# Convolution spectra of a Trainium2 kernel: the last two slices' products and inverses placed beside the down product, and four more slices transformed with eight residues

## The chip, the cores and the metric

The kernel runs on one core of one Trainium2 chip, in one launch. The metric is the device time of that launch in microseconds (us). The engines are named as in the profile: PE (TensorE, matrix products and transposes), DVE (VectorE), ACT (ScalarE), POOL (GpSimd) and SP (SyncE); SP, ACT and POOL also issue DMAs, each from a queue of its own that is worked off in order. PSUM is the memory that PE writes to, and SBUF is where all other tiles lie.

## The reference, cut to what matters

The kernel computes an output and the gradients of nine inputs. S is 2048 rows, D is 1024 columns, F is 3584.

```python
xn = layernorm(q)                              # rows of S x D
k_shift[t] = sum_j k_pad[t + j] * shift_k[.., ks-1-j]   # 4 taps, per column
kv  = k_shift * v
y   = irfft(rfft(kv padded to 2S) * rfft(ssm_k padded to 2S))[:S] + kv * ssm_D
s   = xn_A * y                                 # xn_A is the layer norm again
h   = (xn @ w_gate) * (xn @ w_up)              # S x F
g   = silu(h @ w_down)                         # the "down product"
out = q + s * g
# and the gradients of all inputs but B_x for a given grad_out
```

The long convolution runs column by column over all 2048 rows. The kernel does it as a discrete Fourier transform: PE multiplies pieces of the data by sine and cosine tables, and DVE combines the pieces.

## The kernel before, in words

**Stages.** PE is given one long row of work. First the gate and up products (`gu_unit`, matmuls into `psg` at L671): 14 slabs of 256 columns of F, each in four chunks of four row tiles. Then the down product (`bm_mm`, L1034, into `psbm`): 16 row tiles of 128 rows, each 28 units of two 128x512 matmuls. Then the gradients: `dh_half` (L1482) with `dw_slab` (L1499), `dwd_mm` (L1582) and `dx_part` (L1644).

**The convolution beside them.** `conv_forward` is a generator. It works through eight slices of 128 columns (`ds` 0 to 7) and gives, at each `yield`, an estimate of the DVE time of the piece just recorded. `make_pump` takes from it as much as a planned fraction allows: `tick` is called after each `psg` group and pumps up to a share that grows with a counter over `NT` ticks. So `NT` sets how far the convolution has come at a given chunk of the gate and up products. While `PIN` is set, the DVE instructions stay in the order in which they were recorded.

For a slice the generator does this: transform kv (`transform(ds, 0)`), transform the filter (`transform(ds, 1)`), multiply the spectra (`product`), invert (`inv_dft`, or `inv8` for the slices in `INV8`), and one slice later `tail` does the last matmuls of the inverse (`inv_quad`, L455, two groups per slice into `psI`) and stores the rows into `YFd`. For every two slices `shift` computes `k_shift` and kv; the taps lie broadcast over the partitions in `Wbc`.

**Two forms of the transform.** `fwd4_half` makes PE multiply two residues into each PSUM tile (16 matmuls of 128x256 for a half, 32 for a transform), and DVE needs 8 operations after it. `fwd8_half` multiplies one residue (16 matmuls for a transform) and leaves more butterflies to DVE (`fwd8`, 20 operations). The pairs in `EIGHT` (slice, 0 for kv or 1 for filter) take the second form. In both forms ACT copies `psF` to the tile `SP` and DVE reads it from there.

**What ties PE to DVE in the gate and up stage.** DVE multiplies `gut` to `hN` for each chunk. Some matmul groups later `turn_pair` transposes `hN` on PE (L565), ACT copies the result to `hT`, and SP stores it to `HTd`, from which the down product loads its left operands (`load_ht`, tiles `ht`, or the tiles U10 and U8 for rows 2 and 3). The last of these transposes stand a few us into the down product, on PE's row of work. The load of the last quarter of `w_down` into U9 waits for the store behind them.

**The down product's stage.** Rows 0 and 1 of the down product are recorded first (`bm_first`), then `late_mm(n)` records unit n of the rows from 2 on. At the units in `at`, one step of the convolution's last tail is recorded behind the matmuls, so PE reaches the last inverse matmuls there. Results of rows 2 and 3 are copied by ACT out of PSUM to a tile of the pool `bw` (`bms`), since their gates come later. After `drain()` the rows' gates follow: `gate(b)` is 9 or 10 DVE operations on 128x1024 (so, dgg, gg, sgn, sig, ds_t, dy, dbm, dxa, o_t; rows 0 and 1 have three of them done earlier), 2 sigmoids on ACT and 4 stores of 256 KB on POOL's queue. It needs 3 loads of 256 KB (do_t, xn_t, yf_t) on SP's queue, each into a pair of tiles in turn (`mi`, two buffers), so that the loads of row b+2 wait for the reads of row b. Three PSUM tiles take the rows' matmuls in turn: row b can begin when row b-3 was copied out of PSUM. Copies from row 4 on go to one tile `bm`, which is free when `gg` of the row before has been computed.

Between the row loads SP's queue has the loads of the next `ht` (1.75 MB for two rows of the product) and transposed loads of `DBMd` into the tiles `DBMT` (L1425), which are needed at 700 us. The rows from 12 on have their `dbm` transposed on PE instead (L1323), inside the matmuls of the next row: PE waits there for DVE's `dbm`.

**The end.** `dk_units` uses the taps a second time, beside the last stage of PE.

Of the kernel before, what the change touches and what calls it, by code (L numbers as in the profile page):

```python
# [13 lines left out]
BF16 = mybir.dt.bfloat16  # L14
# [5 lines left out]
def build_kernel(  # L20
# [11 lines left out]
    nc = tc.nc  # L32
# [94 lines left out]
    RSTN = const.tile([P, NB], F32, name="RSTN")  # L127
    Wbc = const.tile([P, 4, D], BF16, name="Wbc")

# [11 lines left out]
    def load_bcast(bsb):  # L141

        wrow = bsb.tile([1, D, 4], BF16, name="wrow")
        st(wrow[:].rearrange("p d j -> p (d j)"), A_shift_k.rearrange("(o d) j -> o (d j)", o=1))
        wtap = bsb.tile([1, 4, D], BF16, name="wtap")

        def turn(j):
            nc.gpsimd.tensor_copy(wtap[:, j, :], wrow[:, :, j])

        def spread():  # L150
            st(WTd.rearrange("(o x) -> o x", o=1), wtap[:].rearrange("p j d -> p (j d)"))
            st(Wbc[:].rearrange("p j d -> p (j d)"), bass.AP(WTd.tensor, WTd.offset, [[0, P], [1, 4 * D]]))
        return turn, spread
# [577 lines left out]
    ht_st = [None]  # L731
    EIGHT = ((0, 0), (0, 1), (6, 0), (7, 0), (7, 1))
    INV8 = (2, 4, 5, 6, 7)
# [6 lines left out]
    def conv_forward():  # L740
        S_ = conv_state

        def load_kv(dp, c):
            S_["k", dp] = krow
            if dp > 0 or c == 0:
                for i in range(2) if dp == 0 else (c,):
                    cld_k(krow[:, i], i, dp)
            if dp > 0 or c == 1:
                for i in range(2) if dp == 0 else (c,):
                    v = U[4][:, 2048 * i:2048 * i + 2048].rearrange("p (a x) -> p a x", a=8)  # L750
                    cld_v(v, i, dp * 256, 256)

        def load_h(ds):
            hrow = U[5][:, 0:2048].rearrange("p (c u r) -> p c u r", c=2, r=8)
            cld(U[5][:, 0:2048], A_ssm_k[ds * P:(ds + 1) * P, :])
            S_["h", ds] = hrow

        def shift(dp):
            kv = cx.tile([P, NB, 256], BF16, name="kv")
            S_["kvt", dp] = kv  # L760
            k = S_.pop(("k", dp))
            wb = lambda j: Wbc[:, j:j + 1, dp * 256:(dp + 1) * 256].unsqueeze(1).to_broadcast([P, 2, 8, 256])
# [12 lines left out]
            yield 2.3  # L775
# [22 lines left out]
        def tail(ds):  # L798
            G = S_.pop(("G", ds))
            if ds < 7:  # L800
                yf = cs.tile([P, NB, P], BF16, name="yf")[:]
            else:
                yf = krow[:].rearrange("p a b d -> p (a b d)")[:, 0:NB * P].rearrange("p (b d) -> p b d", b=NB)
# [63 lines left out]
        for ds in range(8):  # L867
            yield 0.5
            if ds % 2 == 1 and ds < 7:
                with tc.issue_after(S_["kst"].ins):  # L870
                    for c in range(2):
                        load_kv(ds // 2 + 1, c)
            D0 = Dz[:, ds * P:(ds + 1) * P]
            sph = []
            KX = cx.tile([P, 16, 256], BF16, name="KX")
            HX = cs.tile([P, 16, 256], BF16, name="HX", bufs=2)
# [14 lines left out]
            yield from transform(ds, int(ds > 0), sph, HX if ds else KX, room, nop1 if eight else lambda c: h_rows(ds + 1, c),  # L891
                                 behind)
            if ds == 0:
# [14 lines left out]
            sp = []  # L908

            def ahead():  # L910
                if ds < 7:
                    sp.append(half(ds + 1, kvs(ds + 1), len(sp)))
            yield from (inv8 if ds in INV8 else inv_dft)(KX, HX, cs, ahead if ds % 2 == 0 else None, ahead)
            if ds % 2 == 1:
                ahead()
# [65 lines left out]
    cnt = [-5]  # L981
    NT = 24 * 8.0 + 33

# [76 lines left out]

    def load_ht1():
        two_ = [u8(10, a=16), u8(8, a=16)]
        for f0, f1 in ((0, 8), (8, 16), (16, 24), (24, 28)):
            last = ld(two_[f0 // 16][:, f0 % 16:f0 % 16 + f1 - f0], ht_rows(1, f0, f1))
        return (lambda fc: two_[fc // 16][:, fc % 16]), last

    with tc.issue_after(wd_ld.ins):
        ht1 = load_ht1()
# [135 lines left out]
    def dk_units(ew):  # L1204
# [9 lines left out]
        def load_turned(i):  # L1214
# [8 lines left out]
            return kT, dkT  # L1223

        dk = load_rows(0)
        yield 3
        for i in range(16):
            ds, c = divmod(i, 2)
            dsl = slice(ds * P, (ds + 1) * P)
            wb = lambda j: Wbc[:, j:j + 1, dsl].to_broadcast([P, 8, P])  # L1230
            acc = ew.tile([P, 8, P], BF16, name="dka")
# [120 lines left out]
    bm_first(range(fc_, NF))  # L1352
    room = [bw.tile([P, DC, SLW], BF16, name="wdt")[:].rearrange("p (i x) f -> p i (x f)", i=2) for i in range(2)]
    bms = [out_of(pss[i], room[0][:, i]) for i in range(2)]
    first, parts = [u8(q, a=4) for q in (4, 5)]
    y_first[0] = u8(11, a=4)
    with tc.issue_after(ht2[1].ins):
        row_ld[0] = ld(y_first[0][:, :, 0:7 * P], YFd[:, 0:4, 0:7 * P])
    with tc.issue_after(row_ld[0].ins):
# [8 lines left out]
    def late_mm(n):  # L1368
        b, fc = divmod(n, NF)
        b += 2  # L1370
        if fc == 0:
            if 2 < b < 5 and done < 0:
                bms.append(out_of(ps_of[b - 1], room[1][:, b - 3]))
            ps_of[b] = (ps_bx if b % 3 == 2 else ps_bm).tile([P, D], F32, name="psbm")
        with tc.issue_after(inv_mm[0].ins) if b < 5 else nullcontext():
            return bm_mm(ps_of[b], hts[b // 2][0], b % 2, fc)

    at = (62, 69)
    for n in range(at[1] + 1):
        mm = late_mm(n)  # L1380
# [14 lines left out]
    with tc.issue_after(row_ld[0].ins):  # L1395
        ht3 = load_ht(3)
    for i in range(3):
# [8 lines left out]
    rows_in[4] = gate_rows(4, 0, 2) + gate_rows(4, 2, 3, [y_4])  # L1406
    done = at[1] + 1
    while done < 2 * NF:
        late_mm(done)
        done += 1  # L1410
    if len(bms) > 3:
        gate(3, None)
    else:
        gate(3, ps_of[3])
    for bp in range(2, 8):
        hts[bp] = load_ht(bp) if bp > 3 else (ht2, ht3)[bp - 2]
        ht_ld = hts[bp][1]
# [16 lines left out]
        for i in range(2):  # L1434
            n = (2 * bp + i - 2) * NF
            while done < n + NF:
# [371 lines left out]
```

## Time and profile before

| what | value |
|---|---|
| median of 3 runs (lowest to highest) | 1911.96 us (1911.43 to 1912.38) |
| the profiled execution's own time | 1911.63 us |
| its span, first to last instruction | 1909.9 us |
| PE busy | 1899.4 us, 11379 matmuls |
| DVE busy | 1549.7 us |
| gate and up products begin and end on PE | 8.9 and 501.3 us |
| down product begins and ends on PE | 501.2 and 700.2 us |
| granted TensorE clock | 1.000 |

The profile lists instructions by line of the kernel and by the names of the tiles. Matmuls overlap in it: a matmul of 512 columns is listed with 379 ns although the next one starts 216 ns after it, so the cost of one more or one less is read from how far apart the starts of equal matmuls lie. The windows view gives the busy time of each engine in stretches of the span, with the share of time in which the DMA engines were busy and the rate in GB/s. The timeline merges equal instructions that follow one another and puts in brackets how long the engine was idle before and what ended that.

### The profile page before, as it was taken

Reading aid. Unit: us, or ns where it says so; the run is one execution under the profiler, and the core shown is the slowest. Engines: PE = TensorE matmul, PEld = TensorE weight load, DVE = VectorE, ACT = ScalarE, POOL = GpSimd, SP = SyncE. Lnnn points to the kernel's source line nnn. Section 1 sums busy time; section 2 is a strip of 40 time slices with the busy share of each in tenths; the row PEclk is TensorE's granted clock in tenths of the full one; section 3 lists DMA queues with packets and bytes.
Section 4 is the critical chain, followed back from the end, with each engine's and each line's share of the span. In section 5 each row is a group of like instructions: output and inputs, shape, how many; then the busy total and the mean of one; then the engine's idle time right before and its main releaser. Section 6 shows DMA issues by size and latency. Waiting matters only on the chain.

```text
span 1909.9 us, 28150 instructions
## 1 busy us (share of the span) xinstructions
PE 1899.4 (99%) x11379; PEld 1013.9 (53%) x11379; DVE 1549.7 (81%) x1711; ACT 636.8 (33%) x927; POOL 332.7 (17%) x465
## 2 busy tenths in 40 slices
PE   8999999999999999999999999999999999999999
PEld 5555555545444466666666665664444444444444
DVE  8999999999988556887999999999995305788862
ACT  5765555556333233432222222222222102111121
POOL 5121211201113220001031221211212101111120
PEclk9999999999999999999999999999999999999999
DMA  9777766769769997677897798585887999989852
GB/s 298 269 263 233 251 208 223 252 211 311 241 227 307 316 314 231 209 231 233 264 277 247 231 266 258 184 286 180 230 238 181 219 206 190 194 187 190 194 166 88
DMA packets 425106, 444.34 MB, mean 233 GB/s; under 512 B 268400, under 2 KB 342796, under 8 KB 410512
## 3 DMA queue, kind: packets, MB, share of 16 engines
q1 hardware_dynamic: 367504, 239.03, 45.9%
q0 software_dynamic: 41152, 174.15, 29.0%
q10 hardware_dynamic: 16320, 29.36, 4.1%
q8 instruction: 89, 1.46, 0.3%
q14 instruction: 41, 0.34, 0.1%
HBM read 193.87 MB, written 189.84 MB: 201 GB/s over the span
## 4 chain that ended last, share of the span: by engine, by line
PE 97%; DVE 1%; ACT 1%; DMA 0%; issue 0%; SPq 0%; ACTq 0%
PE psb L1499 20%; PE psx L1644 20%; PE psg L671 19%; PE psb L1482 10%; PE psbm L1034 10%; PE psb L1582 9%; PE psF L234 3%; PE psI L455 1%; PE tr L565 1%; PE psY L1193 1%; PE psY L445 1%; PE psx L1582 1%; DVE bst L578 0%; DMA wslab<-in_B_w_gate_dram 0%; PE tr L788 0%; DVE U L212 0%
## 5 line engine op out<-in xcount | busy, mean ns | idle before, releaser
L671 PE MATMUL psg<-wslab,U 128*128 128x512 bf16 x1792 | 401.8, 379 | 3.5 <-DMA wslab<-in_B_w_gate_dram 2.1
L1499 PE MATMUL psb<-U,U 128*128 128x512 bf16 x1792 | 397.1, 379 | 0.0
L1644 PE MATMUL psx<-U,dgut 128*128 128x512 bf16 x1536 | 332.8, 379 | 0.0
L1644 PEld LDWEIGHTS <-dgut 128*128 128x128 bf16 x1792 | 175.3, 98 | 211.4
L1499 PEld LDWEIGHTS <-U 128*128 128x128 bf16 x1792 | 175.2, 98 | 198.0
L671 PEld LDWEIGHTS <-U 128*128 128x128 bf16 x1792 | 172.6, 98 | 197.2 <-issue 3.6
L1482 PE MATMUL psb<-wdt,U 128*128 128x256 bf16 x1792 | 205.6, 273 | 0.0
L1482 PEld LDWEIGHTS <-U 128*128 128x128 bf16 x1792 | 175.2, 98 | 29.2
L212 DVE TENSOR_TENSOR W<-W 128x1024 f32<-128x1024 f32 (+1 forms) x189 | 186.5, 1003 | 4.1
L1582 PE MATMUL psb<-U,U 128*128 128x512 bf16 x816 | 177.3, 379 | 0.0
L1504 ACT CAST wb<-psb 128x512 bf16<-128x512 f32 x112 | 65.6, 586 | 315.4 <-PE psb L1499 310.5
L1249 DVE SCALAR_TENSOR_TENSOR dkp<-dkT,kT 128x1024 bf16<-128x1024 bf16 (+2 forms) x64 | 78.3, 1223 | 93.1 <-DMA dkT<-DKSHd 91.4
L1034 PE MATMUL psbm<-U,ht 128*128 128x512 bf16 x672 | 146.0, 379 | 0.0
L1582 PEld LDWEIGHTS <-U 128*128 128x128 bf16 x896 | 87.4, 98 | 104.4
L673 ACT CAST gut<-psg 128x512 bf16<-128x512 f32 x156 | 91.5, 589 | 120.2 <-PE psg L671 119.7
L1676 ACT ACTIVATE dx_t<-dxn 128x1024 bf16<-128x1024 f32 x15 | 15.9, 1057 | 324.7 <-DVE dxn L212 324.7
L1034 PEld LDWEIGHTS <-ht 128*128 128x128 bf16 x672 | 65.7, 98 | 78.1
L212 DVE TENSOR_TENSOR U<-U,dht 128x2048 bf16<-128x2048 bf16 x56 | 68.3, 1220 | 46.5 <-ACT dht L1484 46.5
L1484 ACT CAST dht<-psb 128x512 bf16<-128x512 f32 x112 | 65.6, 587 | 116.4 <-PE psb L1482 116.4
L66 POOL DMA_DIRECT2D Hd<-hN x54 | 36.6, 677 | 268.9 <-DVE hN L212 258.9
L1623 ACT CAST wbs<-psb 128x512 bf16<-128x512 f32 x51 | 29.9, 586 | 145.4 <-PE psb L1582 134.3
L212 DVE TENSOR_TENSOR W<-SP 128x1024 f32<-128x1024 f32 x64 | 74.1, 1218 | 1.3 <-ACT SP L295 0.8
(263 smaller groups left out, 2342.9 us busy)
## 6 DMA issues: line engine op xcount, KB each, us to landing
U<-GUd SPq DMA_DIRECT2D x28, 1024.0 KB, 9.3
DGd<-U SPq DMA_DIRECT2D x28, 1024.0 KB, 5.8
GUd<-gut ACTq DMA_DIRECT2D x39, 512.0 KB, 5.2
out_dram<-wb SPq DMA_DIRECT2D x112, 128.0 KB, 4.8
U<-Hd SPq DMA_DIRECT2D x14, 1024.0 KB, 6.6
Hd<-hN POOLq DMA_DIRECT2D x54, 256.0 KB, 4.5
HTd<-hT SPq DMA_DIRECT2D x24, 512.0 KB, 3.7
ht<-HTd SPq DMA_DIRECT2D x18, 512.0 KB, 7.5
```

The lines of the kernel that those rows point to most:

```text
L212: pinned(V.tensor_tensor(o, a, b, op))
L234: mm = nc.tensor.matmul(ps[:, k].rearrange("p (c d) -> p c d", c=2), T[:, r, k, :], xr[:, r], start=(n == 0), stop=(n == len(rs) - 1 and ( ...
L671: gu_mm[0] = nc.tensor.matmul(ps[:], XNT[q][:, dc, qi * P:(qi + 1) * P], w[:, dc].rearrange("p a f -> p (a f)"), start=(dc == 0), stop=(dc ...
L673: nc.scalar.copy(out=gut[:, :, i], in_=ps[:].rearrange("p (a f) -> p a f", a=2))
L1034: mm = nc.tensor.matmul(ps[:, dh * 512:(dh + 1) * 512], ht(fc)[:, i * P:(i + 1) * P], WD[fc // 4][:, fc % 4, dh * 512:(dh + 1) * 512], sta ...
L1249: ins = V.scalar_tensor_tensor(prod[:].rearrange("p r d -> p (r d)")[:, lo:H], dkT[:, 0, lo:H], 1.0, kT[:, 0, 13 + m + lo:13 + m + H], op0 ...
L1482: nc.tensor.matmul(ps[:, x * SLW:(x + 1) * SLW], DBMT[2 * hf + g][:, dc, (b % 4) * P:(b % 4 + 1) * P], wdt[:, dc, :], start=(dc == 0), sto ...
L1484: nc.scalar.copy(out=dht[:, 2 * e:2 * e + 2].rearrange("p b f -> p (b f)"), in_=ps[:])
L1499: nc.tensor.matmul(ps[:], XN[b // 4][:, b % 4, dc * P:(dc + 1) * P], dgus[b // 8][:, :, b % 8], start=(b == 0), stop=(b == NB - 1))
L1504: nc.scalar.copy(out=wb[:, dc % 2].rearrange("p a f -> p (a f)"), in_=ps[:])
L1582: nc.tensor.matmul(ps, h[:, f, b, :], DBM[b // 4][:, b % 4, dh * 512:(dh + 1) * 512], start=(b == 0), stop=(b == NB - 1))
L1644: nc.tensor.matmul(ps[:, dh * 512:(dh + 1) * 512], t[n][:, f, i * P:(i + 1) * P], WGU[n][:, f, dh * 512:(dh + 1) * 512], start=(n == 0 and ...
```

## The change

Three things are done.

- The kv transforms of slices 2 to 5 take the form with eight residues (`EIGHT`).
- The loop over slices leaves the products and inverses of slices 6 and 7 out. They follow behind it, product and `inv8` of slice 6, then of slice 7, and both tails come last. Their steps are recorded at four units of the down product (62, 69, 129 and 136 in place of 62 and 69), so the rows' gates begin behind unit 136. `NT` grows by 15. For slice 7 the spectrum and the filter rows lie in the tile of k, which is no longer used then.
- To fit that in: results of rows 2 to 5 are copied to `bw` (three tiles in place of two); the operands of rows 6 and 7 go to U10 and U8 (`load_ht1(3)`); `ht` loads are issued at other places of SP's queue; the broadcast tap tile of all 1024 columns (`Wbc`) is replaced by one of 512 columns (`WB`), refilled on POOL's queue for each later pair of slices, and by four loads `wbk` in `dk_units`; the loads of k and v and the `shift` of the next pair of slices come half a pair earlier.

```diff
-    EIGHT = ((0, 0), (0, 1), (6, 0), (7, 0), (7, 1))
+    EIGHT = ((0, 0), (0, 1), (2, 0), (3, 0), (4, 0), (5, 0), (6, 0), (7, 0), (7, 1))
...
-            st(Wbc[:].rearrange("p j d -> p (j d)"), bass.AP(WTd.tensor, WTd.offset, [[0, P], [1, 4 * D]]))
+            load_taps(WB[:].rearrange("p j e d -> p j (e d)"), 0, 512, ld)
...
+    WB = kst.tile([P, 4, 2, 256], BF16, name="WB")
+
+    def load_taps(t, d0, w, queue=st):
+        queue(t, bass.AP(WTd.tensor, WTd.offset + d0, [[0, P], [D, 4], [1, w]]))
...
         def load_kv(dp, c):
             S_["k", dp] = krow
+            if dp > 1 and c == 0:
+                load_taps(WB[:, :, dp % 2], dp * 256, 256)
...
-                if ds == 7 and rq == 0:
-                    nc.scalar.copy(out=y_first[0][:, 0:4, 7 * P:8 * P], in_=yf[:, 0:4])
+                if ds > 5 and rq == 0:
+                    nc.scalar.copy(out=y_first[0][:, 0:4, ds * P:(ds + 1) * P], in_=yf[:, 0:4])
...
-            if ds % 2 == 1 and ds < 7:
-                with tc.issue_after(S_["kst"].ins):
+            if ds % 2 == 0 and ds < 6:
+                with tc.issue_after(S_["kst"].ins) if ds else nullcontext():
                     for c in range(2):
                         load_kv(ds // 2 + 1, c)
...
                 S_["kst"] = st(KFd[ds], KX[:])
+            if ds % 2 == 1 and ds < 7:
+                yield from shift(ds // 2 + 1)
...
             st(HFd[ds], HX[:])
+            if ds < 6:
+                yield from product(KX, HX, KX, cs, False, 0)
+                yield from (inv8 if ds in INV8 else inv_dft)(KX, HX, cs, ahead if ds % 2 == 0 else None, ahead)
+                if ds % 2 == 1:
+                    ahead()
+                S_["G", ds] = HX
+                tl = tail(ds)
+            else:
+                S_["pair", ds] = (KX, HX)
+                tl = iter(())
+        for ds in (6, 7):
+            KX, HX = S_["pair", ds]
             yield from product(KX, HX, KX, cs, False, 0)
-            if ds % 2 == 1 and ds < 7:
-                yield from shift(ds // 2 + 1)
...
+            yield from inv8(KX, HX, cs, None, None)
             S_["G", ds] = HX
-            tl = tail(ds)
         yield 1e6
-        for _ in tl:
-            yield 1.0
+        for ds in (6, 7):
+            for _ in tail(ds):
+                yield 1.0
...
-    NT = 24 * 8.0 + 33
+    NT = 24 * 8.0 + 48
...
-    bw = pool("bw", 2, side="right")
+    bw = pool("bw", 3, side="right")
...
+            if i % 4 == 0:
+                wbk = ew.tile([P, 4, 256], BF16, name="wbk", bufs=2)
+                load_taps(wbk[:], ds * P, 256)
...
-            if 2 < b < 5 and done < 0:
-                bms.append(out_of(ps_of[b - 1], room[1][:, b - 3]))
+            if 2 < b < 7 and done < 0:
+                bms.append(out_of(ps_of[b - 1], room[(b - 1) // 2][:, (b - 1) % 2]))
...
-        with tc.issue_after(inv_mm[0].ins) if b < 5 else nullcontext():
+        with tc.issue_after(inv_mm[0].ins) if b < 7 else nullcontext():
             return bm_mm(ps_of[b], hts[b // 2][0], b % 2, fc)
-    at = (62, 69)
-    for n in range(at[1] + 1):
+    at = (62, 69, 129, 136)
+    for n in range(at[-1] + 1):
+        if n == 2 * NF:
+            hts[3] = load_ht1(3)
+        if n == 4 * NF:
+            hts[4] = load_ht(4)
         mm = late_mm(n)
...
     with tc.issue_after(row_ld[0].ins):
-        ht3 = load_ht(3)
+        hts[5] = load_ht(5)
...
-    done = at[1] + 1
-    while done < 2 * NF:
-        late_mm(done)
-        done += 1
-    if len(bms) > 3:
-        gate(3, None)
-    else:
-        gate(3, ps_of[3])
+    done = at[-1] + 1
+    gate(3, None)
     for bp in range(2, 8):
-        hts[bp] = load_ht(bp) if bp > 3 else (ht2, ht3)[bp - 2]
+        if bp in (5, 6):
+            hts[bp + 1] = load_ht(bp + 1)
...
-            gate(2 * bp + i, ps_of[2 * bp + i])
+            gate(2 * bp + i, ps_of[2 * bp + i] if 2 * bp + i >= len(bms) else None)
```

More of the change, by code (lines that the diff above doesn't have):

```diff
@@ L127, in build_kernel @@
     RSTN = const.tile([P, NB], F32, name="RSTN")
-    Wbc = const.tile([P, 4, D], BF16, name="Wbc")
     tip = tc.alloc_tile_pool(name="tip", bufs=1)
@@ L753, in load_h @@
         def load_h(ds):
-            hrow = U[5][:, 0:2048].rearrange("p (c u r) -> p c u r", c=2, r=8)
-            cld(U[5][:, 0:2048], A_ssm_k[ds * P:(ds + 1) * P, :])
-            S_["h", ds] = hrow
+            room = (U[5][:] if ds < 7 else krow[:].rearrange("p a b d -> p (a b d)"))[:, 0:2048]
+            cld(room, A_ssm_k[ds * P:(ds + 1) * P, :])
+            S_["h", ds] = room.rearrange("p (c u r) -> p c u r", c=2, r=8)
         def shift(dp):
@@ L761, in shift @@
             k = S_.pop(("k", dp))
-            wb = lambda j: Wbc[:, j:j + 1, dp * 256:(dp + 1) * 256].unsqueeze(1).to_broadcast([P, 2, 8, 256])
+            wb = lambda j: WB[:, j:j + 1, dp % 2].unsqueeze(1).to_broadcast([P, 2, 8, 256])
             room = cx.tile([P, 16, 256], BF16, name="KX")[:].rearrange("p a x -> p (a x)") if dp == 0 else U[7][:]
@@ L874, in conv_forward @@
             sph = []
-            KX = cx.tile([P, 16, 256], BF16, name="KX")
+            if ds < 7:
+                KX = cx.tile([P, 16, 256], BF16, name="KX")
+            else:
+                KX = krow[:].rearrange("p a b d -> p (a b d)")[:, 0:4096].rearrange("p (a x) -> p a x", a=16)
             HX = cs.tile([P, 16, 256], BF16, name="HX", bufs=2)
@@ L890, in conv_forward, with ahead, rows_on @@
             room = cf.tile([P, 4, 256], F32, name="room", tag="hx")[:] if eight else None
-            yield from transform(ds, int(ds > 0), sph, HX if ds else KX, room, nop1 if eight else lambda c: h_rows(ds + 1, c),
-                                 behind)
+            sp = []
+            def ahead():
+                sp.append(half(ds + 1, kvs(ds + 1), len(sp)))
+            def rows_on(c):
+                if not eight:
+                    h_rows(ds + 1, c)
+                if ds == 6:
+                    ahead()
+            yield from transform(ds, int(ds > 0), sph, HX if ds else KX, room, rows_on, behind)
             if ds == 0:
@@ L904, in conv_forward @@
             st(HFd[ds], HX[:])
-            yield from product(KX, HX, KX, cs, False, 0)
-            if ds % 2 == 1 and ds < 7:
-                yield from shift(ds // 2 + 1)
[L908 to L915, printed above, removed]
+            if ds < 6:
+                yield from product(KX, HX, KX, cs, False, 0)
+                yield from (inv8 if ds in INV8 else inv_dft)(KX, HX, cs, ahead if ds % 2 == 0 else None, ahead)
+                if ds % 2 == 1:
+                    ahead()
+                S_["G", ds] = HX
+                tl = tail(ds)
+            else:
+                S_["pair", ds] = (KX, HX)
+                tl = iter(())
+        for ds in (6, 7):
+            KX, HX = S_["pair", ds]
+            yield from product(KX, HX, KX, cs, False, 0)
+            yield from inv8(KX, HX, cs, None, None)
             S_["G", ds] = HX
-            tl = tail(ds)
         yield 1e6
-        for _ in tl:
-            yield 1.0
+        for ds in (6, 7):
+            for _ in tail(ds):
+                yield 1.0
         cs.release()
@@ L1059, in build_kernel, with load_ht1 @@
         wd_ld = load_wd(j)
-    def load_ht1():
+    def load_ht1(bp):
         two_ = [u8(10, a=16), u8(8, a=16)]
         for f0, f1 in ((0, 8), (8, 16), (16, 24), (24, 28)):
-            last = ld(two_[f0 // 16][:, f0 % 16:f0 % 16 + f1 - f0], ht_rows(1, f0, f1))
+            last = ld(two_[f0 // 16][:, f0 % 16:f0 % 16 + f1 - f0], ht_rows(bp, f0, f1))
         return (lambda fc: two_[fc // 16][:, fc % 16]), last
     with tc.issue_after(wd_ld.ins):
-        ht1 = load_ht1()
+        ht1 = load_ht1(1)
     fc_ = 8
@@ L1223, in load_turned @@
             return kT, dkT
+        wbk = None
         dk = load_rows(0)
@@ L1229, in dk_units @@
             dsl = slice(ds * P, (ds + 1) * P)
-            wb = lambda j: Wbc[:, j:j + 1, dsl].to_broadcast([P, 8, P])
+            if i % 4 == 0:
+                wbk = ew.tile([P, 4, 256], BF16, name="wbk", bufs=2)
+                load_taps(wbk[:], ds * P, 256)
+            wb = lambda j: wbk[:, j:j + 1, ds % 2 * P:(ds % 2 + 1) * P].to_broadcast([P, 8, P])
             acc = ew.tile([P, 8, P], BF16, name="dka")
@@ L1352, in build_kernel @@
     bm_first(range(fc_, NF))
-    room = [bw.tile([P, DC, SLW], BF16, name="wdt")[:].rearrange("p (i x) f -> p i (x f)", i=2) for i in range(2)]
+    room = [bw.tile([P, DC, SLW], BF16, name="wdt")[:].rearrange("p (i x) f -> p i (x f)", i=2) for i in range(3)]
     bms = [out_of(pss[i], room[0][:, i]) for i in range(2)]
@@ L1357, in build_kernel @@
     with tc.issue_after(ht2[1].ins):
-        row_ld[0] = ld(y_first[0][:, :, 0:7 * P], YFd[:, 0:4, 0:7 * P])
+        row_ld[0] = ld(y_first[0][:, :, 0:6 * P], YFd[:, 0:4, 0:6 * P])
     with tc.issue_after(row_ld[0].ins):
```

5 lines of the change are left out of this document (1 added, 4 removed).

## The prediction

> **What bounds the kernel now.** I read the page's busy times and slices first, for the engine that is never idle.
>
> ```profile
> PE 1899.4 (99%) x11379; PEld 1013.9 (53%) x11379; DVE 1549.7 (81%) x1711; ACT 636.8 (33%) x927; POOL 332.7 (17%) x465
> ...
> PE   8999999999999999999999999999999999999999
> DVE  8999999999988556887999999999995305788862
> ...
> DMA  9777766769769997677897798585887999989852
> ```
>
> A slice is 47.7 us. PE is full throughout, and the chain of waits gives PE 97% of the span, so a matmul that goes is time gained wherever nothing else is late. But DVE is full too in slices 1 to 10, the gate and up products, and has room only in the down product (slices 11 to 14), where the DMA engines are busy. How close the two are is seen where PE needs DVE's last `hN`, in the timeline:
>
> ```profile
> 504.61 1.04 PE L455 MATMUL psI<-HX,TI 128*128 128x256 bf16 x8
> ...
> 505.22 0.68 DVE L212 TENSOR_TENSOR hN<-gut 128x1024 bf16<-128x1024 bf16 x1
> ...
> 509.03 0.64 PE L565 MATMUL tr<-ident,hN 64*128 64x64 bf16 x32
> ```
>
> DVE ends `hN` at 505.90 and PE transposes it at 509.03: the slack is 3.1 us. A PE that comes earlier by more than that waits. Next, the down product's stage, in timelines of DVE, SP and PE:
>
> ```profile
> 597.25 0.69 DVE L212 TENSOR_TENSOR so<-xn_t,yf_t 128x1024 bf16<-128x1024 bf16 x1 [4.12 <-DMA yf_t<-YFd]
> ...
> 668.57 0.68 DVE L212 TENSOR_TENSOR dbm<-dgg,sig 128x1024 bf16<-128x1024 bf16 x1
> ```
> ```profile
> 586.41 0.32 SPq L61 DMA_DIRECT2D yf_t<-YFd  x1
> ...
> 603.58 9.29 SPq L1425 DMA_TRANSPOSE U<-DBMd  x1
> ```
> ```profile
> 670.65 0.61 PE L1323 MATMUL tr<-ident,dbm 128*128 128x128 bf16 x8
> ```
>
> Row 6's gate waited for a load issued 10.8 us before; a transposed load holds SP's queue for 9.3 us; and PE takes row 12's `dbm` 1.4 us after DVE made it (669.25). These are the covers that the change uses up.
>
> **The change, part by part.** All times are set against the profiled execution (1911.63 us with 1909.9 of span, so 1.7 lies around it; the median, 1911.96, is 0.3 above it, and I take the difference from the median).
>
> *Matmuls, gain 7.0.* Four transforms go from 32 to 16 matmuls of 128x256: 64 fewer, which is what the changed program's order shows (22760 PE rows become 22632, half of them weight loads). Equal matmuls of this size start 0.109 apart (eight in 1.04 with a last one of 0.273: 0.77 / 7). 64 x 0.109 = 7.0. The groups view's busy time would give more (25.5 / 208 = 0.123, 7.8), but it counts the overlapping end of each run, so I keep 7.0.
>
> *DVE in the gate and up stage, cost 2.4.* A transform of the old form takes 358.03 to 367.12, 9.1 us; one of the new form 427.93 to 444.99 without two `hN` of 0.6, 15.85. Four times 6.75 is 27.0 added. Product and inverse of one slice (slice 7's, 520.62 to 548.48) are 27.9, and one such pair, slice 6's, leaves the work ahead of the last `hN`. So DVE does only 0.9 less there, while PE does 7.0 less and one `psI` run of 0.87 moves behind the transposes. PE is ready at 509.03 - 7.87 = 501.2, `hN` at 505.9 - 0.9 = 505.0: PE waits 3.8. DVE had three waits of 0.3 to 0.6 on ACT's `gut` (1.4 in all after 120 us), which vanish if PE runs ahead of it. That leaves 2.4; bounds 0 (DVE has 4.7 idle in all between 120 and 506) and 4.5 (more operations, more small gaps). Net at this point: 4.6.
>
> *Inverses beside the down product, nothing.* Behind the last `hN`, DVE needs 14 + 27.9 to the end of slice 6: 504.3 + 42 = 546.3; PE comes there at 554.95 less 4.6, 550.3, and only 28 us after that to slice 7, whose work takes 27.9 and ends at 574.2 against PE's 580. Each has some 4 us of cover; without it the lateness is paid in full.
>
> *Gates 24.3 later, cost 1.5.* They begin when PE has done the last `psI`. That was 559.9; now 67 more units of 0.432 (28.9) stand ahead, less 4.6: 584.2. A gate is 6.1 on DVE, a row of matmuls 12.1, so DVE can catch up, if its loads come. Two points can hold PE. First, row 10's matmuls need row 7 copied out of PSUM, behind row 6's `gg`. Row 4's last read of yf_t is at 586.4 + 24.3 = 610.7; with the median landing of yf_t, 7.4, row 6 starts at 618.1, `gg` ends 1.3 later, the copy (1.0) at 620.5; PE comes at 501.15 + 125.1 - 4.6 = 621.7. Held by 1.2. Second, row 12's `dbm`. Row 8 starts at 631.1 (618.1 + 5.5 + 7.4). Behind its loads the transposed load keeps SP until 633.4, so row 9's loads land at 642; row 10 follows at 648.1, its loads ahead of the second transposed load; row 11 at 654.9. Row 12's yf_t goes out at 653.6 with 1.75 MB of `ht` ahead: row 12 starts at 661 to 664 and `dbm`, ninth in its order, ends 5.5 later, 666.5 to 669.5. PE is there at 670.65 - 4.6 = 666.1, so it waits 0.4 to 3.4. Since a wait here lets later rows off, I take 1.5; bounds 0 (loads in the shortest 3.7) and 9.3 (the slowest, 10.7, below). By row 14 the gates are level, and the last transposed load (669 before) goes out by then, so the next stage starts as before.
>
> *Bandwidth, weighed once.* The windows view shows both ends:
>
> ```profile
> 590.00:600.00 10.00, 10.00 (x48) 4.53 (x47) 5.75 (x11) 3.02 (x3) 2.51 (x4) 1.00 0.95 365
> ...
> 660.00:680.00 20.00, 20.00 (x101) 9.31 (x99) 8.98 (x15) 7.04 (x7) 2.53 (x4) 1.00 1.02 255
> ```
>
> The last two columns are DMA share and GB/s. A gate row moves seven times 256 KB and half a row of `ht`, 2.3 MB: 6.3 us at 365 GB/s, 9.0 at the 255 seen with a transposed load in flight. [...]
>
> *The rest, nothing.* The first tap load is half as large, on SP's queue at about 34.5 behind an `HTd` store; `Wbc` landed in 7.5 and its first reader starts at 51.1. If late, DVE pays it all. `wbk` is issued a unit of work ahead, where DVE idles 74.3 at once for dkT; uncovered, four landings of 7.5 on an idle engine. The refills of `WB` and the earlier k and v loads wait on POOL for DVE reads that lie behind them in the order too, so `Hd` stores behind them wait no longer than now. U9's load (515.42, needed at 524.6) follows the last hT store, which moves with PE's transposes: cover of some 2.6 kept. Two ACT copies replace one (0.6).
>
> Sum: -7.0 + 2.4 + 1.5 = -3.1, **1908.9 us**; with the middle parts of the bounds 1907 to 1911.
>
> **Rivals.**
> *All of it is gained.* DVE's small idle times shrink and loads land early: -7.0 to -5.0, 1905 to 1907. For: DVE's 4.7 of idle. Against: its work ahead of the last `hN` hardly falls.
> *Almost nothing is gained.* DVE 3.8 late and `dbm` 2 to 6 late: -1 to +3.8, 1911 to 1915.8. For: row 6's 10.8 us landing.
> *Slower: loads pace the gates.* At the slowest landing, 10.7, two rows take 5.5 + 10.7 = 16.2, as a row's loads wait for the row two before. Row 6 starts at 621.4, row 12 at 670.0, `dbm` at 675.5, 9.4 behind PE: -7.0 + 2.4 + 9.4 = +4.8, 1916.8. It decides once `dbm` is later than 4.6. For: the share of 1.0 and above from 610 on. Against: `ht` loads for rows 8 to 11 now go out before 590, not among these rows.
> *The change doesn't take effect:* excluded by the order, which has the 64 fewer matmuls and 48 more DVE operations.
>
> **How the numbers follow.** Forecast 0.50 (1907 to 1911), all gained 0.18, almost nothing 0.20, slower 0.12. A measurement of this kernel tells 0.2%, 3.8 us, from no change: below 1908.1 is faster. Of the forecast's 0.50 some 0.22 lies there, with 0.18 that is 0.40 faster; 0.28 + 0.20 = 0.48 within; 0.12 slower. The range of 1905.3 to 1914 leaves out the slower rival and the ends.
>
> **What would show it.** PE L234 on kv: 144 matmuls in place of 208. At the last transposes of `hN` PE idles 2 to 4 us on DVE; were there no wait, the DVE step is wrong. `psI` of slices 6 and 7 without a wait. The first gate at about 584; row 6 waiting for yf_t; PE idle ahead of row 10's first matmul or of row 12's `dbm`, 0 to 3 us in all, with DVE level with PE from row 13 or 14. The prediction is wrong if PE waits elsewhere in the gate and up stage, if U9 or `ht` comes late, or if the last stage's DVE waits reach PE.

## The result, and the profile after

The changed kernel takes 1939.72 us (median of 5 runs, 1938.14 to 1944.69) against 1911.96 (1911.43 to 1912.40): a ratio of 1.0153, 95% interval 1.0135 to 1.0170. It is 27.8 us slower, and outside the range that was forecast. The profiled execution has a span of 1937.9 us, 28.0 more than that of before. First the page's busy times, slices and chain of waits:

```profile
span 1937.9 us, 28067 instructions
...
PE 1896.4 (98%) x11315; PEld 1007.8 (52%) x11315; DVE 1575.1 (81%) x1759; ACT 637.4 (33%) x928; POOL 337.3 (17%) x470
...
PE   8999999999999869999999999999999999999999
...
DVE  8999999999997545888799999999996205788862
...
PE 69%; DVE 19%; DMA 5%; issue 5%; ACT 1%; POOL 1%; SPq 0%; DVEq 0%; POOLq 0%; ACTq 0%
```

PE is now idle for part of slices 14 and 15 (630 to 727 us), the later part of the down product, and the chain gives it 69% where it had 97. The waits view (engine and line, what it waited for, total us, times, longest) names the wait:

```profile
PE tr L1346 <- DVE dbm L211: 21.2, 2, 20.5
PE psbm L1053 <- ACT bm L1291: 2.4, 2, 2.1
PE psg L674 <- ACT gut L676: 2.3, 3, 1.2
...
PE psbm L1053 <- DMA ht<-HTd: 1.9, 1, 1.9
```

One wait of 20.5 us is three quarters of the loss: PE stands ahead of row 12's transposes until DVE has made `dbm`, in PE's timeline:

```profile
665.97 8.36 PE L1053 MATMUL psbm<-U,ht 128*128 128x512 bf16 x38 [0.32 <-ACT bm L1291]
694.82 1.03 PE L1346 MATMUL tr<-ident,dbm 128*128 128x128 bf16 x8 [20.49 <-DVE dbm L211]
```

Why `dbm` was late is read one engine further back, in DVE's timeline. The first operation of rows 8, 9 and 12, and what DVE waited for ahead of it:

```profile
639.70 0.69 DVE L211 TENSOR_TENSOR so<-xn_t,yf_t 128x1024 bf16<-128x1024 bf16 x1 [2.75 <-DMA yf_t<-YFd]
...
663.52 0.69 DVE L211 TENSOR_TENSOR so<-xn_t,yf_t 128x1024 bf16<-128x1024 bf16 x1 [17.72 <-DMA yf_t<-YFd]
...
689.01 0.69 DVE L211 TENSOR_TENSOR so<-xn_t,yf_t 128x1024 bf16<-128x1024 bf16 x1 [7.10 <-DMA yf_t<-YFd]
```

DVE stood idle for 17.7 us ahead of row 9, for a load. SP's queue shows why that load was late:

```profile
630.23 0.32 SPq L61 DMA_DIRECT2D yf_t<-YFd  x1
630.72 15.62 SPq L1447 DMA_TRANSPOSE U<-DBMd  x1
...
648.83 0.96 SPq L61 DMA_DIRECT2D yf_t<-YFd  x1
```

The first transposed load (into U10) held the queue for 15.6 us, where the like of it had held it for 9.3. Row 9's loads were issued behind it. From issue to landing the DMA view gives (stretch from 630.5 to 638 us; engine, count, KB each, median us):

```profile
out_dram<-o_t POOLq DMA_DIRECT2D x2, 256.0 KB, 14.9
yf_t<-YFd SPq DMA_DIRECT2D x1, 256.0 KB, 9.3
DYd<-dy POOLq DMA_DIRECT2D x1, 256.0 KB, 21.0
U<-DBMd SPq DMA_TRANSPOSE x1, 28.2
```

In the kernel before the same load took 14.3, and the stores beside it 6.3 to 9.1 (stretch from 602 to 612 us):

```profile
DYd<-dy POOLq DMA_DIRECT2D x2, 256.0 KB, 6.3
...
out_dram<-o_t POOLq DMA_DIRECT2D x2, 256.0 KB, 9.1
...
U<-DBMd SPq DMA_TRANSPOSE x1, 14.3
```

Both the transposed load and the stores beside it are slow: a store of 256 KB took 21 us. The windows view (DMA share and GB/s last; a share above 1 means that the packets' times add up to more than the 16 engines' time) shows a share of 1.10 to 1.32 and, from 640 us on, only some 100 GB/s:

```profile
635.00:640.00 5.00, 5.00 (x25) 2.27 (x24) 2.25 (x5) 1.75 (x2) 2.51 (x4) 1.00 1.10 336
640.00:645.00 5.00, 5.00 (x25) 2.25 (x23) 5.00 (x9) 2.43 (x3) 0.70 (x1) 1.00 1.32 101
645.00:650.00 5.00, 5.00 (x25) 2.25 (x23) 0.81 (x2) 0.69 (x1) 1.81 (x4) 1.00 1.29 100
```

The remaining loss lies in the gate and up stage. Timelines of PE and ACT, and a line of the windows view whose third number from the end is the granted clock:

```profile
436.60 0.41 PE L568 MATMUL tr<-ident,hN 64*128 64x64 bf16 x16 [0.92 <-DVE hN L211]
438.17 3.55 PE L674 MATMUL psg<-wslab,U 128*128 128x512 bf16 x8 [1.16 <-ACT gut L676]
```
```profile
437.53 1.07 ACT L676 CAST gut<-psg 128x512 bf16<-128x512 f32 x2 [5.02 <-DMA GUd<-gut]
```
```profile
439.00:441.00 2.00, 2.00 (x6) 0.73 (x5) 2.00 (x1) 1.44 (x2) 0.00 (x0) 0.50 1.15 347
```

ACT waited 5.0 us before it could overwrite a `gut` tile whose store had not landed. That store lay in a heap of transfers issued between 423 and 428 us (two pieces of `w_down`, two `wslab`, `HFd`, `YFd`); PE idled twice, and then ran at half clock: 6 matmuls in 2 us where 9 fit at one every 216 ns.

Where the 28.0 us of span are, by stage (lengths from the first matmul of one stage to that of the next):

| stage | before | after | difference | of which |
|---|---|---|---|---|
| gate and up products | 492.2 | 490.9 | -1.3 | -7.0 fewer matmuls, +5.7 waits and half clock |
| down product | 198.9 | 226.6 | +27.7 | waits of 25.5 in the lines above; half clock behind them and small gaps |
| gradients, to the last instruction | 1209.8 | 1211.5 | +1.7 | a wait of 1.2 for `XNd` |

### The profile page after: what moved, and what is told of

It reads as the page before. It is cut to its first block, busy times and chain, and to the rows that moved or that the text cites. A ratio compares the mean times of both kernels' runs of the same rounds, so it can differ in the third digit from the quotient of the medians.

```text
span 1937.9 us, 28067 instructions
## 1 busy us (share of the span) xinstructions
PE 1896.4 (98%) x11315; PEld 1007.8 (52%) x11315; DVE 1575.1 (81%) x1759; ACT 637.4 (33%) x928; POOL 337.3 (17%) x470
## 4 chain that ended last, share of the span: by engine, by line
PE 69%; DVE 19%; DMA 5%; issue 5%; ACT 1%; POOL 1%; SPq 0%; DVEq 0%; POOLq 0%; ACTq 0%
PE psx L1666 20%; PE psb L1521 20%; PE psb L1504 9%; PE psb L1604 9%; DVE W L211 6%; PE psbm L1053 5%; DVE HX L211 3%; DVE KX L211 2%; PE psg L674 2%; DMA yf_t<-YFd 2%; DVE U L211 2%; DVE m L211 1%; DVE hN L211 1%; DMA U<-XNd 1%; PE psF L233 1%
## 5 line engine op out<-in xcount | busy, mean ns | idle before, releaser
L211 DVE TENSOR_TENSOR W<-W 128x1024 f32<-128x1024 f32 (+1 forms) x201 | 196.9, 995 | 4.4
L1053 PE MATMUL psbm<-U,ht 128*128 128x512 bf16 x560 | 123.5, 381 | 4.3 <-ACT bm L1291 2.4
L1053 PEld LDWEIGHTS <-ht 128*128 128x128 bf16 x560 | 55.0, 99 | 70.5 <-issue 4.3
```

Of the source, the lines that this page charges most:

```text
L211: pinned(V.tensor_tensor(o, a, b, op))
L1053: mm = nc.tensor.matmul(ps[:, dh * 512:(dh + 1) * 512], ht(fc)[:, i * P:(i + 1) * P], WD[fc // 4][:, fc % 4, dh * 512:(dh + 1) * 512], sta ...
```

## The experiments

Three theories were set against each other. Theory A: a transposed load is slow while stores of POOL's queue run beside it; the late gates, which run 6.1 us apart in place of 12, bring that about, and the loads of rows 9 to 12 lie behind it on SP's queue. Theory B: the gates start too late, and their loads, whichever they are, cannot catch up. Theory C: DVE's heavier transforms are the cause.

**1. The moved products alone.**

```diff
-    EIGHT = ((0, 0), (0, 1), (2, 0), (3, 0), (4, 0), (5, 0), (6, 0), (7, 0), (7, 1))
+    EIGHT = ((0, 0), (0, 1), (6, 0), (7, 0), (7, 1))
```

> The changed kernel with the kv transforms of slices 2 to 5 back in the old form, so that only the moved products and inverses, the loads and the copies are left of the change. Theory A (the loss sits in the down product's stage: gates 27 us later, their loads stuck behind a transposed load that the gates' own stores slow down): PE does 7.0 more, the waits of the gate and up stage (2.4 on hN and 1.6 at a halved clock behind it) go, and the wait of 20.7 us ahead of row 12's transposed dbm stays within 5 us of that: 1936 to 1947 us. Theory C (the loss comes from the heavier transforms on DVE): without them the kernel is back at 1910 to 1918 us.

Measured 1941.90 us (ratio 1.0163, 1.0146 to 1.0180), and PE's wait is there unchanged:

```profile
697.92 1.03 PE L1346 MATMUL tr<-ident,dbm 128*128 128x128 bf16 x8 [20.75 <-DVE dbm L211]
```

Theory C falls: the loss comes with the moved products, and with or without the new transforms the time is the same within the intervals.

**2. The new transforms alone.** In the kernel before, `EIGHT` gets the four pairs, and `NT` ends in 29 in place of 33.

> The kernel before with the kv transforms of slices 2 to 5 in the new form and nothing moved (NT from 33 to 29 in its last term, so that the filters are still done in time). 64 matmuls go, 7.0 us. DVE gets 27.0 more ahead of the last hN, with 3.1 of slack there and 4.7 of idle time: PE, 7 earlier, waits 7 + 27 - 3 - 4 = 27 on DVE in the gate and up stage, so 1928 to 1935 us, and no wait beyond 3 us in the down product's stage. If DVE had hidden room (rival), 1905 to 1912 us.

Measured 1939.52 us (1.0146, 1.0130 to 1.0161), 4.5 over the upper end of what was expected. The down product begins at 530.2 us in place of 501.2. The waits view has the largest waits where kv is made; those at `hN` come to 3.1 us:

```profile
PE psF L234 <- DVE kv L212: 14.5, 3, 6.3
PE psF L234 <- ACT SP L295: 4.7, 3, 4.1
```

So DVE has no hidden room in that stage, and each half of the change costs 28 to 30 us alone.

**3. The transposed loads later.** U10 behind row 12's loads, the first slab behind row 13's, U8 behind row 14's, U4 and the second slab behind row 15's.

```diff
-            if bp in (4, 5, 7):
-                q = (4, 5, 7).index(bp)
+            if bp in (6, 7):
+                q = bp - 6
...
+                    nc.sync.dma_start_transpose(out=DBMT[2], in_=DBMd[1024:1536, :])
```

> The changed kernel with the transposed loads of DBMd put later in SP's queue: U10 behind row 12's loads, U8 behind row 14's, U4 and both w_down slabs behind row 13's and 15's. Theory A: with no transposed load among them, rows 9 to 12 follow one another at 6 to 7.5 us from 645 on, dbm of row 12 is there at 669 to 675, and PE's wait ahead of its transposes falls from 20.7 to 0 to 3 us; some of it may come back at the start of the next stage, where PE needs U10, U8, U4 and the first slab (0 to 12 us): 1915 to 1932 us. Theory B (the loads of seven 256 KB pieces and half a row of ht for each gate row are themselves too slow for gates that start so late): rows 9 to 12 stay 10 us or more apart, the wait stays above 12 us, 1932 us or more.

Measured 1946.12 us, from 1933.07 to 1953.82 (1.0173, 1.0125 to 1.0221). The part that tells A from B came out for A: `dbm` of rows 9 to 11 ended at 651.3, 657.5 and 663.6, 6.1 apart, so the gates do catch up when no transposed load is among them. PE's wait for row 12 fell to 6.6. The time came out in the range that was named for B, but not in B's way: the same slow loads now stood ahead of the next stage, and PE lost more there than the 12 us that A had allowed. U4's, beside ten stores, took 31.8 us from issue to landing:

```profile
734.25 8.73 PE L1506 MATMUL psb<-wdt,U 128*128 128x256 bf16 x64 [14.22 <-DMA U<-DBMd]
```

**4. Stores of rows 8 to 11 on SP's queue**, where they are issued in turn with the transposed loads.

```diff
-        st(DBMd[b * P:(b + 1) * P, :], dbm)
+        put = ld if 8 <= b < 12 else st
+        put(DBMd[b * P:(b + 1) * P, :], dbm)
```

(and so for the other three stores)

> The changed kernel with the four stores of each of rows 8 to 11 issued on SP's queue in place of POOL's, so that they can't run beside the transposed loads of U10 and U8, which are on SP's queue. Theory A with the stores as what slows the transposed load: U10 lands 4 to 8 us behind the load ahead of it (19.4 in the changed kernel), row 9's gate starts at 648 to 653 in place of 663.5, and the wait ahead of row 12's transposes falls from 20.7 to 5 to 12 us: 1924 to 1932 us. Rival (the transposed load is slow for another reason, its place or its rows): U10 takes 15 us or more again and the time stays within 4 us of 1939.7, or rises by the stores that now lie in SP's queue.

Measured 1937.63 us (1.0130, 1.0104 to 1.0157): by the words of the expectation the rival's side. U10 landed 17.7 us behind the load ahead of it and PE waited 19.9. But row 7's four stores were still on POOL's queue, issued from 635.5 on, and each took 21 us. So U10 still had stores of another queue beside it, and the next run moves those too.

**5. Stores of rows 6 to 11 on SP's queue.** `put = ld if 6 <= b < 12 else st`.

> As the run with rows 8 to 11 stored on SP's queue, but rows 6 to 11, since there the transposed load of U10 still had row 7's stores on POOL's queue beside it (they landed 21 us after their issue, and U10 27 us after its own). Theory A (stores that run beside it slow the transposed load): with no store on POOL's queue while U10 is read, it lands 4 to 6 us behind what is ahead of it on SP's queue. Rival (it is slow wherever it stands here): 15 us or more. On the time nothing is certain, as SP's queue now has 24 stores among the loads and ht comes later: 1920 to 1940 us.

Measured 1934.33 us (one time, so without an interval). With no store on another queue beside it U10 landed in 8.3 us from its issue (28.2 in the changed kernel), 3.7 behind the load ahead of it, and row 9's gate had next to no wait. DMA view of the stretch from 633 to 641 us, then DVE's and PE's timelines:

```profile
U<-DBMd SPq DMA_TRANSPOSE x1, 8.3
```
```profile
649.40 0.69 DVE L211 TENSOR_TENSOR so<-xn_t,yf_t 128x1024 bf16<-128x1024 bf16 x1 [0.32 <-DMA yf_t<-YFd]
```
```profile
686.98 1.04 PE L1347 MATMUL tr<-ident,dbm 128*128 128x128 bf16 x8 [4.15 <-DVE dbm L211]
...
732.37 1.89 PE L1522 MATMUL psb<-U,U 128*128 128x512 bf16 x4 [6.25 <-DMA U<-XNd]
```

PE's wait for row 12 is down from 20.5 to 4.2. Part of it comes back in the next stage, where `XNd` lies behind the last transposed loads, slow again beside the stores of rows 12 to 15.

**6. Late transposed loads, and rows 6 to 15 stored on SP's queue** (3 and 5 together).

> The order of the run with late transposed loads, with the stores of rows 6 to 15 on SP's queue, so that no store runs beside a transposed load. Theory A: each of the five transposed loads (U10, slab 0, U8, U4, slab 1) lands 3 to 6 us behind the load ahead of it, where with POOL's stores U10 took 13, U8 12 and U4 21; the 14.4 us that PE waited at the start of the next stage fall to 0 to 6; 1915 to 1930 us. Rival: the transposed loads stay at 11 us or more, 1933 us or more.

Measured 1935.95 us (one time). All five transposed loads took 3.3 to 4.2 us behind the load ahead of them, as theory A has it; the time did not follow. PE waited 4.7 for row 12 and then 10.2 for `A<-DYd`, which needs the last rows' stores, now at the end of a full SP queue.

**7. Rows 8 to 11 transposed by PE**, so that U4's load goes; U10 behind row 12's loads, the first slab behind row 13's, U8 behind row 14's.

```diff
-        if b >= 12:
+        if b >= 8:
             defer(turn)
...
```

> The changed kernel with rows 8 to 11 transposed by PE too (32 matmuls of 128x128, 1.8 us), so that U4's transposed load goes, and U10's and U8's behind row 12's and row 14's loads with slab 0 behind row 13's. Theory A: row 12's dbm comes at 664 to 680 and U8 lands near 709 instead of U4 at 734: PE's waits fall from 21.5 + 2 to 8 to 15 in all, 1922 to 1933 us. Theory B (gates too late in themselves): 1935 us or more.

Measured 1944.64 us, 1932.66 to 1949.79 (1.0151, 1.0117 to 1.0185); expected were 1922 to 1933. A transpose on PE puts a wait for `dbm` into PE's row: 5.2 us for row 8 at 644, 2.8 at 696. U10, U8 and the second slab took 12 to 15 us beside 8 stores, and PE waited 17.0 us for `XNd` behind them.

**8. Plain loads in place of the transposed ones** for U10 and U8, in the same places. The kernel leaves out the transposition of rows 0 to 7, so only its time can be used.

```diff
-                dma_t = nc.sync.dma_start_transpose(out=DBMT[q], in_=DBMd[512 * q:512 * q + 512, :])
+                if bp == 7:
...
+                else:
+                    dma_t = ld(u8((10, 8)[q], a=4), DBMd[512 * q:512 * q + 512, :].rearrange("(b u) d -> u b d", u=P))
```

> The changed kernel with U10 and U8 loaded plainly from the same rows of DBMd, 1 MB each, in the same places of SP's queue, and not transposed (the products of rows 0 to 7 with w_down in the backward pass are thus of wrong operands; nothing else is changed). Theory A: a plain 1 MB takes 3 to 8 us, row 9's gate starts at 648 to 652 in place of 663.5, dbm of row 12 is there at 669 to 678, the wait of 20.7 us falls to 0 to 5: 1916 to 1925 us. Theory B (not the transposed loads, but the sum of the gates' loads is too slow): 1930 us or more.

Measured 1924.74 us (1.0070, 1.0055 to 1.0085), within what theory A expected. The stores beside a plain load of 1 MB land in 7 to 9 us and the load itself 4.6 to 5.1 behind the one ahead. Row 9 starts at 647.4, row 12 at 672.0, and PE waits 5.8, a little over the 0 to 5 expected:

```profile
647.36 0.69 DVE L211 TENSOR_TENSOR so<-xn_t,yf_t 128x1024 bf16<-128x1024 bf16 x1 [1.50 <-DMA yf_t<-YFd]
```
```profile
677.77 1.04 PE L1346 MATMUL tr<-ident,dbm 128*128 128x128 bf16 x8 [5.84 <-DVE dbm L211]
```

So of the 27.8 us some 15 are that these two loads transpose.

**9. Another pace.** `NT` ends in 44 in place of 48.

> The changed kernel with NT ending in 44 in place of 48, so that the convolution runs a little faster beside the gate and up products and its stores and the w_down loads fall on other chunks. In the changed kernel PE lost 2.4 us there at 435 to 438, with a gut store that took 8 to 12 us in a heap of 1 MB transfers, and 1.6 more at a halved clock behind the wait. Theory: the wait is that collision; elsewhere in the order the two terms go (0 to 1 us left at 425 to 445) and the down product's stage loses its 20 us all the same: 1934 to 1942 us. Rival (DVE is too late there whatever the pace): 2 to 6 us of waits on hN or gut stay in the gate and up stage.

Measured 1945.06 us (1.0181, 1.0163 to 1.0199), above the theory's range and nearer the rival. The wait on the `gut` store is down to 0.3, but waits of 0.7 to 1.8 us stand at 302, 323, 381, 441 and 457, most of them on ACT's copies of `psF` and not, as the rival had it, on `hN` or `gut`; the down product begins at 504.8, later than in both kernels. The collision was one place where a stage without slack gave way, not the cause.

**10. Rows 6 to 13 stored on SP's queue, the second slab behind the XN loads.**

> As the run with rows 6 to 11 stored on SP's queue, but rows 6 to 13, and the second w_down slab's transposed load behind the XN loads in place of ahead of them. Theory A: U10, U8 and U4 take 3.7 to 4.5 us each; the 11.2 us that PE waited for XN at the start of the next stage fall to 0 to 4; ahead of row 12's transposes 2 to 6 us stay: 1918 to 1926 us. If the stores in SP's queue hold up the loads by as much as they free (rival), 1930 us or more.

Measured 1931.80 us, 1926.11 to 1940.41 (1.0108, 1.0072 to 1.0144). U10, U8 and U4 take 3.7 us each, as expected; the wait for `XNd` falls to 1.7, but 3.0 for `A<-DYd` and 4.4 for row 12 stay, with half clock behind them. The median is 2 us inside the rival's range, the lowest time at the edge of A's; the terms that A named came out as named (`XNd` 0 to 4, row 12 2 to 6), and what it had left out are `DYd` and the half clock.

**11. The kernel before, with rows 5 to 13 stored on SP's queue.**

> The kernel before with the stores of rows 5 to 13 on SP's queue in place of POOL's; nothing of the change is in it. In the kernel before the transposed loads with stores beside them took 11.1 (U10), 7.6 (slab 0) and 10.6 us (U4), and those without 3.5 and 1.7. Theory A: without stores on POOL's queue all three fall to 2 to 5 us, and the time stays where it is (1910 to 1914 us), since the kernel before hides them: its rows are 12 us apart, and a load that lands 10 us late is still in time. Rival (their length there has another cause): they stay at 7 us or more. If the time rises by over 4 us, SP's queue with 36 stores in it is itself the limit, and the runs with stores on SP's queue understate what the transposed loads cost.

Measured 1912.11 us (1.0001, 0.9991 to 1.0010). The loads of U10, the first slab and U4 took 6.1, 1.9 and 3.7 us behind the load ahead, where they had taken 11.1, 7.6 and 10.6 (U10 is 1 above what was expected). So the kernel before has the same contention and hides it, and 36 stores in SP's queue cost it nothing.

**12. As 10, with the `ht` loads for rows 14 and 15 behind row 12's loads.**

> As the run with rows 6 to 13 stored on SP's queue and the second slab behind XN, and the ht loads for rows 14 and 15 (1.75 MB) behind row 12's loads in place of ahead of them. Theory: of PE's last wait ahead of row 12's transposes (4.5 us, with 3.4 us lost to a halved clock behind it) most was the ht ahead of row 12's loads; the wait falls to 0 to 2 us: 1918 to 1925 us. Rival (the gates are simply that late, by DVE and the stores in SP's queue): the wait stays at 4 us or more, 1926 us or more.

Measured 1934.01 us (1.0109, 1.0093 to 1.0125). Row 12's `dbm` came at 681.9 in place of 685.9, and PE had no wait for it, but waited 4.5 for those `ht` loads instead, and 8.9 for `A<-DYd` (3.0 in run 10). The wait came out as the theory had it, the time as the rival: these loads together are late by that much, whichever of them comes first.

The transposed loads into U10, U8 and U4 (1 MB each) from all these runs and from the kernels before and after, by the time from the landing of the load ahead on SP's queue (or the own issue, if later) to the own landing, and by the POOL stores of 256 KB that were under way meanwhile:

| stores beside it | loads | us |
|---|---|---|
| none | 13 | 3.6 to 4.2, one 6.1 |
| 2 to 5 | 13 | 3.5 to 7.8, one 17.7 |
| 7 or 8 | 9 | 10.3 to 14.6, one 6.9 |
| 9 or 10 | 4 | 15.4 to 20.8 |

The counts are in part an effect, since a load that takes long meets more stores. Counted when the load's turn comes, as the stores that are then still under way for 0.3 us or more, the order is the same: none for 21 loads of 3.5 to 6.1 us, one to three for 8 of 5.8 to 11.6, four for 10, nine of them of 11.5 to 20.8 and one of 6.9 (run 5). That the stores are a cause, and not only a companion, rests on run 5, which took them away. In run 4 the four stores of row 7 alone were enough for 17.7.

## Why the prediction was wrong

*Matmuls, gain 7.0.* Right: 64 fewer (144 on kv at L233), 7.0 us at 0.109 from one start to the next.

*DVE in the gate and up stage, cost 2.4.* The size was too small and the place wrong. The last transposes of `hN`, where the wait was to be, had none (PE was there at 506.83); the stage had lost 5.7 more than before by then: 0.8 at 83, 2.4 from 435 to 438, 1.6 by half clock up to 441, 1.2 at 478 and small gaps (all by the starts of matmuls, which gives 0.1 to 0.3 more for a wait than the idle time in the views), while the kernel before loses 0.8 at one place between 80 and 500. Only one slack was worked out, that of the last `hN`; run 9 shows that the stage gives way in many places; DVE had 4.7 us of idle time in all there in the kernel before.

*Inverses beside the down product, nothing.* Right: `psI` of slices 6 and 7 had no wait.

*Gates 24.3 later, cost 1.5: the step that failed.* The start was nearly right: PE had done the last `psI` at 587.5 (584.2 forecast) and held 2.1 us for row 7's copy (1.2 forecast). The failing sentence is "Behind its loads the transposed load keeps SP until 633.4, so row 9's loads land at 642". It kept SP until 646.3, and row 9's last load landed at 663.1. The 9.3 us of queue, and the 14.3 to landing behind it, were taken from one row of the kernel before, as if they belonged to the load. They belonged to the load and to the stores beside it. Why it took 19.4 us behind the load ahead here and 11.1 there is not shown: 7 stores overlapped it there and 9 here, but four of the nine, row 8's, were issued 4.7 to 6.7 us after its turn had come, and run 4, which issues those four on SP's queue behind the load, still took 17.7. So row 7's four stores are enough, and that the gates follow one another in 6.1 us (theory A) is not shown to be the reason. Runs 3 and 8 show that without this wait rows 9 to 11 follow one another as forecast, and run 5 that row 9 comes at 649.4; run 11 shows that the price was in the profile of before already, paid where nobody waited. For the term of 1.5 the stage of the down product paid 27.7 in all.

A second, smaller step failed ahead of this one. Row 8's gate began at 639.7 where 631.1 was forecast, before the transposed load had its turn: PE's last `psI` came 3.3 late, and DVE waited 4.2 for row 4's `xn_t` and 2.8 for row 8's `yf_t`. The prediction had the `ht` loads for rows 8 to 11 "go out before 590, not among these rows"; SP's queue was with them until 597.9, and row 4's loads were issued behind them, as timelines of SP and DVE show:

```profile
574.97 22.89 SPq L61 DMA_DIRECT2D ht<-HTd  x8
597.90 2.25 SPq L61 DMA_DIRECT2D yf_t<-YFd  x2
```
```profile
612.42 0.69 DVE L211 TENSOR_TENSOR so<-xn_t,yf_t 128x1024 bf16<-128x1024 bf16 x1 [4.17 <-DMA xn_t<-XNd]
```

No run moves these `ht` loads, so what they cost is not measured.

*The bounds, 0 to 9.3.* The upper end took the slowest landing of a plain load (10.7). The same view of before had the transposed loads' own times side by side: 14.3, 10.8 and 14.0 from issue, that is 11.1, 3.5 and 10.6 behind the load ahead. A time that varies threefold within one profile is not a constant to be carried over, and this spread was not asked for its cause.

*The slower rival* had the right mechanism (loads pace the gates, and `dbm` decides once it is 4.6 late) and the right side, with 9.4 us in place of 20.5, and was given 12%; it too was priced by a plain load's landing. *Bandwidth, weighed once:* the lowest rate weighed was 255 GB/s, and the changed kernel moved 100 from 640 to 650 us; row 12's wait of 20.5 is over twice the upper bound of 9.3. POOL's stores do slow SP's transposed load (U10 landed 28.2 us after its issue with them, 8.3 in run 5 without), and most of that comes with the transposition: run 8's plain 1 MB beside like stores took 5.1 us where the transposed one took 19.4.

*The rest, nothing.* Nearly: `ht` for row 12 came 1.9 late, `XNd` 1.2, an `hT` copy 1.1 (the one at 478 above); the tap loads and U9 cost nothing.

Of the 27.8 us, then: -7.0 by matmuls, +5.7 in the gate and up stage, some +15 by two transposed loads beside stores (run 8), and about +14 by gates that are late in themselves, theory B's part (4 to 6 us of wait for row 12 in runs 5, 8 and 10), the smaller waits and the half clock behind them. The last is what remains, and is not measured by itself. No version of the change tried here came below 1911.96.

## What to carry to other kernels

A DMA's time in a profile belongs to its company (U10 took 19.4 us behind the load ahead with stores beside it, 3.7 in run 5 without): before moving work, ask what ran beside each transfer that the plan relies on, and whether the move brings it other company; a spread between equal transfers of one profile (3.5 to 11.1 us in that of before) is the warning. Work that is moved into an engine's free time also moves its transfers, and a burst that catches up doubles the rate of its stores (here a row's four every 6.1 us from 623 to 636, where the kernel before has them every 12.1 from 631 to 668) just where the slack has been spent. Where a transposed load must meet stores, put both on one queue: that cut the load from 28 to 8 us here (run 5), though the time of the whole fell by only 5 to 8 us (runs 5 and 10), since other waits took the place of this one.

## What the runs showed of the hardware

**A transposed load and plain stores slowed each other far more than their bytes.** Alone, 1 MB mostly took 3.7 us (some 280 GB/s); beside 9 or 10 stores of 256 KB 15 to 21 us, with the DMA engines of the changed kernel at a share of 1.3 and 100 GB/s (640 to 650 us). Row 7's four stores took 21 us there, and stores 7 to 9 beside run 8's plain load. Alone the transposed load was no slower than that plain 1 MB, which took 4.6 to 5.1 with stores beside it. The number of stores doesn't give the time: with four under way when the load's turn came it took from 6.9 (run 5) to 20.8 us (run 3), and what sets it within that stays open.

**Half clock after short waits.** From 694 to 696 us, behind the wait of 20.5, the granted clock was 0.50, and 0.50 from 439 to 441, behind waits of 0.92 and 1.16 us that ended 1.6 us apart, while one of 2.1 us at 625 left the clock at 1.00. So the length of a single wait did not decide it, and what did is not shown.

**The times of kernels whose PE waits for DMAs, or for a DVE that does, spread more here.** The five times of the changed kernel lie within 6.6 us and the four of run 3 within 20.8, against 1.0 for the kernel before, whose PE hardly waits for a DMA (2.1 us in all), and 2.0 for run 2, whose PE waits mostly for DVE and ACT. That the waits are the reason was not tested.
